# x's first 512 rows loaded as row pairs and transposed as even and odd tiles, with one filler slot fewer, in a dense GELU forward and backward kernel

## The chip, the cores and the metric

The kernel runs on one core of one Trainium2 chip. The metric is the device time of one execution in microseconds (us); a time of a kernel is the median of several runs. A profiled execution also gives a span, from the first to the last instruction of the program.

## The reference

A dense layer with tanh-GELU, its output, and the gradients of all five inputs for a given `grad_out`:

```python
def _fwd_reference(x, w1, b1, w2, b2):
    h = jnp.einsum("bsd,df->bsf", x, w1) + b1
    h = jax.nn.gelu(h, approximate=True)
    return jnp.einsum("bsf,fd->bsd", h, w2) + b2
# B, S, D, F = 1, 2048, 448, 1792, all bf16
# outputs: out, and the vjp at grad_out: dx, dw1, db1, dw2, db2
```

## The kernel before

The 2048 rows of x are worked in 4 blocks of 512 rows, the 1792 hidden columns in 14 tiles of 128, two of which form a pair; so there are 28 pairs (block, two hidden tiles). For each pair TensorE (PE) computes u = (x w1) transposed, VectorE (DVE) and ScalarE (ACT) add the bias and make GELU and its derivative, PE computes q = (grad_out w2^T) transposed, DVE multiplies the two. PE also makes the rows of the output (`o`) and of dx (`x`) from earlier pairs. When all pairs are done, PE computes dw1 (line 843) and dw2 (line 897) with full-height matmuls; everything before runs as two half-height matmuls of 64 rows side by side, a slot (line 246).

The order on every engine is written out by hand, in the strings `PE_ORDER`, `ACT_ORDER`, `DVE_ORDER` and `SP_ORDER`. A planner (`Plan`) walks these five lists and emits an instruction when all that it needs has been emitted; the waits themselves are put in afterwards by the framework, from the memory that each instruction reads and writes, in the order of emission.

The first 512 rows of x need to stand transposed in `xT[0]`, 64 columns of edge and then one column for each row of x. For the other blocks a transposing DMA does that. For the first block the rows are loaded plainly (`LXN`, tokens `xr..`, into the tile `TR2`), PE transposes them by a matmul with an identity (`XT`, tokens `X0` to `X3`, four slots each, into the PSUM banks 0 to 3), and DVE and ACT copy the results out of PSUM into `xT[0]` (`XC`, line 637). A token `X2.1` in `DVE_ORDER` or `ACT_ORDER` is the copy of tile 2, half 1; a half is 64 of the tile's 128 rows. Tiles 0 and 2 use banks 0 and 1, tiles 1 and 3 use banks 2 and 3, so X2 can't be transposed before the copies of X0 are done.

PE's program begins

```python
W6 X0 X1 F6 X2 X3 S0 B T1 u1.1 h1.2 u1.2 u2.1 ...
```

- `W6`: six matmuls of 512 columns on a constant (line 393), which need no data.
- `X0 X1`: transposes of tiles 0 and 1.
- `F6`: six slots of 128 columns on a constant (`fill`), which write PSUM banks that nobody reads.
- `X2 X3`: transposes of tiles 2 and 3.
- `S0`: pair 0's u for columns 0 to 255 of the block, 14 matmuls of 256 columns in 7 slots. It reads the columns of xT that tiles 0 and 1 fill, and the first part of w1.
- `B`: a small matmul that turns b1 (line 711). DVE copies its result (token `b1T`, line 736), and all bias additions need it.
- `T1`: pair 0's u for columns 256 to 511, first half of its sum, in two pieces of 128 columns. It reads what tiles 2 and 3 fill.

The loads are issued at the very start: tile 0 on SP's queue (`xr01`), tile 1 on ACT's (`xr12`), tiles 2 and 3 together on SP's (`xr24`), then parts of w1 on both.

Where ACT and DVE share the copies: DVE has X0.0, X1.0, X2.1, X3.1, ACT has X0.1, X1.1, X2.0, X3.0.

Of the kernel before, what the change touches and what calls it, by code (L numbers as in the profile page):

```python
# [88 lines left out]


PE_ORDER = """
W6 X0 X1 F6 X2 X3 S0 B T1 u1.1 h1.2 u1.2 u2.1 u3.1 u2.2 u3.2 p0.0 p0.1 p0.2 p0.3 p1.0 p1.1 p1.2 u4.1 u5.1 u4.2
u5.2 p1.3 p2.0 p2.1 p2.2 p2.3 u6.1 p3.0 u6.2 p3.1 p3.2 p3.3 p4.0 p4.1 u7.1 p4.2 u7.2 p4.3 p5.0 p5.1 p5.2 p5.3 u8.1
p6.0 u8.2 q0.1 p6.1 q0.2 u9.1 p6.2 u9.2 q1.1 p6.3 q1.2 u10.1 o1.0.0.6.1 u10.2 q2.1 o1.1.0.6.1 u11.1 q2.2 u11.2
o1.0.0.6.2 o1.1.0.6.2 q3.1 u12.1 q3.2 u12.2 o1.0.6.10.1 q4.1 o1.1.6.10.1 u13.1 q4.2 u13.2 o1.0.6.10.2 q5.1 o1.1.6.10.2
# [43 lines left out]
@with_exitstack  # L139
def kernel(  # L140
    ctx: ExitStack,
    tc: tile.TileContext,
    x: bass.AP,
    w1: bass.AP,
    b1: bass.AP,
    w2: bass.AP,
    b2: bass.AP,
    grad_out: bass.AP,
    out_0: bass.AP,
    out_1: bass.AP,  # L150
    out_2: bass.AP,
    out_3: bass.AP,
    out_4: bass.AP,
    out_5: bass.AP,
):
    pl = make_plan(tc, ctx, x, w1, b1, w2, b2, grad_out, out_0, out_1, out_2, out_3, out_4, out_5)
    with tc.manual_schedule():
        pl.emit()


def make_plan(tc, ctx, x, w1, b1, w2, b2, grad_out, out_0, out_1, out_2, out_3, out_4, out_5):
    nc = tc.nc
    P = 128
    _, S, D = x.shape
# [5 lines left out]
    EDGE = 64  # L170
    sc = math.sqrt(GELU_C * GELU_A)

    x2 = x.rearrange("b s d -> (b s) d")
# [19 lines left out]
    xT = [sb.tile([P, 4, EDGE + SB], BF16, name=f"xT{i}") for i in range(2)]  # L193
# [9 lines left out]
    NUB, NUX, NTR = 3, 14, 3  # L203
    ub_t = [sb.tile([P, 2, SB], BF16, name=f"ub{i}") for i in range(NUB)]
    ub_x = [gh_nat[:, NB - 1 - i // NPB, 2 * (i % NPB):2 * (i % NPB) + 2, :, :].rearrange("p f s c -> p f (s c)") for i in range(NUX)]
    TR = [sb.tile([P, 2, 2, SB], BF16, name=f"TR{i}") for i in range(NTR)]
# [10 lines left out]
    def bk_(i):  # L217
        return BK[i][:, :] if i < 6 else qb[:, i - 6, :]
# [8 lines left out]
    def bk16(i):  # L227
        return bk_(i)[:, 0:D].bitcast(BF16)
# [186 lines left out]
    def val(v, place):  # L415
        if v not in pl.place:
            pl.put(v, place)
        return v
# [135 lines left out]
    def dq(eng):  # L554
        return {"SP": nc.sync, "ACT": nc.scalar, "POOL": nc.gpsimd}[eng]
# [4 lines left out]
    def dma(eng, name, out, in_, reads, writes, nbytes):  # L560
        def fn():
            d = loads[name] = dq(eng).dma_start(out=out, in_=in_)
            if name in HOLD:
                tc.add_manual_dep(d.ins, loads[HOLD[name]].ins.name, DEP, reason="behind the identity")
        pl.op(eng, name, fn, list(reads) + (["ident"] if name in HOLD else []), writes, ("dma", nbytes, "plain"))
# [27 lines left out]
        pl.op("DVE", f"edge{tag}", lambda: nc.vector.tensor_copy(out=dst[64:128, 3, EDGE - 1:EDGE], in_=dst[0:64, 0, EDGE:EDGE + 1]),  # L593
              [(tag, 0, 0)], [v], ("tiny", 1))

    x_rows = TR[NTR - 1][:, :, :, :].rearrange("p a h s -> p (a h) s")
    ident = stage[0][:, 0, 0:P]
    nums, turned, nums128 = stage[1][:, 0, 0:16], stage[1][:, 0, 32:64], stage[1][:, 0, 128:256]
    row, block = [stage[1][:, 1, 2 * i:2 * i + 2].bitcast(F32) for i in (0, 1)]

    def LXN(t0, t1, eng="SP"):

        src = x2[t0 * P:t1 * P, :].rearrange("(t p) d -> p t d", p=P)
        dma(eng, f"xrows{t0}", x_rows[:, t0:t1, 0:D], src, [], [("xrows", t) for t in range(t0, t1)], (t1 - t0) * 114688)

    def identity():

# [24 lines left out]
        pe(f"xt{t}", fn, [("xrows", t), "ident"], [bank(("xt", t, i), bks[i]) for i in (0, 1)], ("s64", 4), (bks, 0))  # L632

    def XC(t, i, eng):
        out = xT[0][:, :, EDGE + t * P + 64 * i:EDGE + t * P + 64 * i + 64]
        src = bk16(X_BANKS[t][i])[:, 0:256].rearrange("p (k s) -> p k s", k=4)
        fn = (lambda: nc.scalar.copy(out=out, in_=src)) if eng == "ACT" else (lambda: nc.vector.tensor_copy(out=out, in_=src))
        pl.op(eng, f"xc{t}.{i}", fn, [("xt", t, i)], [val(("xT", 0, t // 2), ("xT", 0, t // 2))], ("copy", 256))
# [56 lines left out]
    def num(t):  # L695
        return [int(i) for i in t.split(".")]

    for t in PE_ORDER.split():
        k, a = t[0], t[1:]
# [15 lines left out]
        elif k == "h":  # L715
            hf, d = num(a)
# [7 lines left out]
        else:  # L724
            b, half, f0, f1, d = num(a)
# [13 lines left out]
    for eng, order in (("ACT", ACT_ORDER), ("DVE", DVE_ORDER)):  # L739
        for t in order.split():  # L740
            k, a = t[0], t[1:]
            if k == "k":
                CS(0, "AB".index(a[-1]))
            elif k == "c":
                hf = None if a[-1] in "AB" else int(a[-1])
                a = a if hf is None else a[:-1]
                C(int(a[:-1]), "AB".index(a[-1]), eng, hf)
            elif k == "v":
                EV(a[0], *num(a[1:]), eng)
            elif k == "L":  # L750
                LW1(int(a), eng)
            elif k == "Z":
                LW1Z(int(a), eng)
            elif t[:2] == "xr":
                LXN(int(t[2]), int(t[3]), eng)
            elif t == "ident":
                pl.op(eng, "ident", identity, ["identz"], ["ident"], ("tiny", 1))
            elif k == "X":
                XC(*num(a), eng)
            elif k == "D":  # L760
                LED({"x": "xT", "g": "gT"}[a[0]])
            elif k == "K":
                LW2(int(a), eng)
            elif t in ("b1", "b2"):
                (LB1 if t == "b1" else LB2)(eng)
            elif t == "b1T":
                pl.op(eng, "b1T", b1_turn, [("b1u",)], ["b1T"], ("tiny", 4))
            elif t == "table":
                pl.op(eng, "table", lambda: nc.scalar.activation(out=tiny[:], in_=one[:, 0:1], func=ACT.Gelu_apprx_tanh), [], ["tiny"], ("table", 1))
            else:  # L770
                step[k](int(a))
# [7 lines left out]
    for t in SP_ORDER.split():  # L779
        k, a = t[0], t[1:]  # L780
        if t[:2] == "xr":
            LXN(int(t[2]), int(t[3]), "SP")
        elif k in "XY":
            b, *hs = num(a)
            LX(*((x2, xT, "xT") if k == "X" else (g2, gT, "gT")), b, hs or [0, 1])
        elif k in "RF":
            (LW1R if k == "R" else LW1F)()
        elif t in ("b1", "b2"):
            (LB1 if t == "b1" else LB2)("SP")
        elif t in ("L1a", "L1b"):  # L790
            LW1(1, "SP", *((0, 2) if a[-1] == "a" else (2, 3)))
        elif k in "LZKJI":
            {"L": LW1, "Z": LW1Z, "K": LW2, "J": LW2T, "I": LW1T}[k](int(a))
        elif k == "E":
            LE("SP")
        elif k in "HT":
            {"H": HS, "T": GHT}[k](int(a))
        elif k == "S":
            ST(a[0], *num(a[1:]))
        elif t == "Nx":  # L800
            rows_nat("xn", x_nat, x2, [("w1", i) for i in range(len(W1_COLS))] + ["w1r", "w1f"])
        elif t == "Ng":
            rows_nat("gn", g_nat, g2, [("w2T", i) for i in range(4)])
# [34 lines left out]
    for ft in range(NF):  # L838
# [7 lines left out]
        eng = "ACT"  # L846
        dst, src = w_stage[ft % (4 * NTR)][:, 0:D], bk_(bk)[:, 0:D]
# [4 lines left out]
        c = ft // 4  # L852
# [37 lines left out]
    for ft in range(NF):  # L890
        halves = [(0, D)] if ft < NF - 1 else [(0, D - P), (D - P, D)]
        for (d0, d1) in halves:
# [7 lines left out]
            dst, src = gw2_sb[:, ft, d0:d1], bk_(bk)[:, 0:d1 - d0]  # L900
            eng = "DVE" if (ft % 2 == 1 and ft < NF - 1) else "ACT"
# [39 lines left out]
```

## Time and profile before

| | us |
|---|---|
| median of 3 runs | 263.89 |
| lowest, highest run | 263.8, 264.7 |
| the profiled execution, its own time | 264.0 |
| its span | 262.2 |
| PE busy in the span | 258.8 |
| DVE busy | 199.0 |
| ACT busy | 127.7 |

The two timestamps that matter are inside the first 7 us: the transposes of x begin at 3.41 us of the span, and the first real matmuls of u at 4.89 us. From there to the end PE always has an instruction in work. Ends of matmuls in the profile are modelled, and one matmul's end lies beyond the start of the next, so the pace of PE is read from starts.

### The profile page before, as it was taken

Reading aid. Unit: us, or ns where it says so; the run is one execution under the profiler, and the core shown is the slowest. Engines: PE = TensorE matmul, PEld = TensorE weight load, DVE = VectorE, ACT = ScalarE, POOL = GpSimd, SP = SyncE. Lnnn points to the kernel's source line nnn. Section 1 sums busy time; section 2 is a strip of 40 time slices with the busy share of each in tenths; the row PEclk is TensorE's granted clock in tenths of the full one; section 3 lists DMA queues with packets and bytes.
Section 4 is the critical chain, followed back from the end, with each engine's and each line's share of the span. In section 5 each row is a group of like instructions: output and inputs, shape, how many; then the busy total and the mean of one; then the engine's idle time right before and its main releaser. Section 6 shows DMA issues by size and latency. Waiting matters only on the chain.

```text
span 262.2 us, 5414 instructions
## 1 busy us (share of the span) xinstructions
PE 258.8 (99%) x2217; PEld 148.2 (57%) x2217; DVE 199.0 (76%) x287; ACT 127.7 (49%) x166; POOL 14.2 (5%) x11
## 2 busy tenths in 40 slices
PE   8999999999999999999999999999999999999995
PEld 5544455555555666666666676765555555555554
DVE  4998398999989989999997995249999999310000
ACT  4899569936898956875896310011121111000001
POOL 1000000000000000000000000000000392400000
DMA  7999989999999982972488725875899799974221
GB/s 211 287 262 161 196 130 198 249 338 223 254 180 232 254 179 43 193 206 43 109 201 258 214 42 63 249 221 116 176 212 174 157 231 153 232 158 128 72 70 35
DMA packets 120617, 46.61 MB, mean 178 GB/s; under 512 B 96670, under 2 KB 120463, under 8 KB 120592
## 3 DMA queue, kind: packets, MB, share of 16 engines
q1 hardware_dynamic: 119904, 45.82, 77.3%
q10 hardware_dynamic: 688, 0.44, 0.5%
q8 instruction: 17, 0.28, 0.4%
q14 instruction: 8, 0.07, 0.1%
HBM read 8.20 MB, written 14.28 MB: 86 GB/s over the span
## 4 chain that ended last, share of the span: by engine, by line
PE 99%; ACT 0%; issue 0%
PE bank L246 48%; PE qb L246 18%; PE bank L843 16%; PE bank L897 16%; PE qb L393 1%; ACT w_sb L902 0%; PE bank L711 0%
## 5 line engine op out<-in xcount | busy, mean ns | idle before, releaser
L246 PEld LDWEIGHTS <-HG 64*128 64x128 bf16 x896 | 54.7, 94 | 33.1 <-POOLq L239 2.1
L246 PE MATMUL qb<-gT,w2Tf 64*128 64x512 bf16 x392 | 52.8, 376 | 0.0
L246 PE MATMUL bank<-w_sb,HG 64*128 64x448 bf16 x448 | 48.3, 349 | 0.0
L246 PE MATMUL bank<-xT,w1f 64*128 64x512 bf16 (+2 forms) x361 | 47.2, 367 | 0.0
L246 PE MATMUL bank<-w1T_sb,HG 64*128 64x448 bf16 x448 | 47.2, 349 | 0.0
L519 DVE SCALAR_TENSOR_TENSOR HG<-TR,qb 128x1024 bf16<-128x1024 bf16 x28 | 34.1, 1216 | 12.6 <-PE qb L246 12.6
L897 PE MATMUL bank<-w2Tf,HG 128*128 128x448 bf16 (+2 forms) x240 | 42.6, 340 | 0.0
L843 PE MATMUL bank<-w1f,gh_nat 128*128 128x448 bf16 x224 | 42.5, 352 | 0.0
L897 PEld LDWEIGHTS <-HG 128*128 128x128 bf16 x240 | 22.9, 98 | 19.8
L843 PEld LDWEIGHTS <-gh_nat 128*128 128x128 bf16 x224 | 21.8, 98 | 20.6 <-issue 0.4
L246 PEld LDWEIGHTS <-w2Tf 64*128 64x128 bf16 x392 | 23.6, 94 | 17.1 <-POOLq L239 0.3
L504 ACT ACTIVATE TR<-TR 128x1024 bf16<-128x1024 bf16 x28 | 29.2, 1052 | 6.6 <-DVE TR L494 6.6
L246 PEld LDWEIGHTS <-w1f 64*128 64x128 bf16 x388 | 22.1, 95 | 16.9 <-POOLq L239 0.7
L866 DVE TENSOR_TENSOR w1T_sb<-w1T_sb,gh_nat 128x1792 f32<-128x1792 f32 x14 | 28.4, 2026 | 0.5
L848 ACT ACTIVATE TR<-bank 128x448 bf16<-128x448 f32 x14 | 7.6, 544 | 34.9 <-PE bank L843 34.9
L903 DVE CAST w_sb<-bank 128x448 bf16<-128x448 f32 x6 | 3.7, 624 | 25.9 <-PE bank L897 25.9
L902 ACT CAST w_sb<-bank 128x448 bf16<-128x448 f32 (+2 forms) x9 | 4.4, 491 | 37.7 <-PE bank L897 37.7
L872 POOL PARTITION_ALL_REDUCE w1T_sb<-w1T_sb x1 | 10.6, 10568 | 205.9 <-DVE w1T_sb L870 205.9
L479 ACT ACTIVATE TR<-gh_nat 128x1024 bf16<-128x1024 bf16 x15 | 15.7, 1052 | 11.5 <-DVE TR L514 11.5
L509 DVE TENSOR_SCALAR TR<-TR 128x2048 bf16<-128x2048 bf16 x28 | 19.1, 687 | 1.9 <-ACT TR L504 1.9
L499 DVE TENSOR_TENSOR TR<-TR,HG 128x1024 bf16<-128x1024 bf16 x28 | 19.1, 682 | 0.0
L514 DVE TENSOR_TENSOR TR<-TR 128x1024 bf16<-128x1024 bf16 x28 | 19.0, 684 | 0.1
(54 smaller groups left out, 190.4 us busy)
## 6 DMA issues: line engine op xcount, KB each, us to landing
hT_dram<-HG SPq DMA_DIRECT2D x28, 256.0 KB, 3.1
out_dram<-st SPq DMA_DIRECT2D x16, 224.0 KB, 3.1
w1f<-in_x_dram SPq DMA_DIRECT2D x2, 896.0 KB, 5.8
w2Tf<-in_grad_out_dram SPq DMA_DIRECT2D x1, 1792.0 KB
out_dram<-w_sb SPq DMA_DIRECT2D x2, 448.0 KB, 3.0
out_dram<-xT SPq DMA_DIRECT2D x2, 384.0 KB, 3.8
w_sb<-in_w_dram SPq DMA_DIRECT2D x1, 672.0 KB
w1f<-in_w_dram SPq DMA_DIRECT2D x3, 192.0 KB, 3.6
```

What stands on the lines that cost most here:

```text
L246: m = nc.tensor.matmul(out, lhsT=l, rhs=r, start=st, stop=sp, skip_group_check=True, is_transpose=turn or None)
L479: pl.op("ACT", f"s{p}", lambda: nc.scalar.activation(out=TR[p % NTR][:, 1], in_=ubuf(p), func=ACT.Square, scale=sc), [("ub", p)], [v], ("a ...
L499: pl.op("DVE", f"R{p}", lambda: nc.vector.tensor_tensor(out=t[:, 1], in0=t[:, 1], in1=hblk(p), op=ALU.mult), [("r", p), ("h", p)], [val((" ...
L504: pl.op("ACT", f"t{p}", lambda: nc.scalar.activation(out=t[:, 0], in_=t[:, 0], func=ACT.Tanh), [("y", p)], [val(("t", p), ("TR0", p % NTR) ...
L509: pl.op("DVE", f"m{p}", lambda: nc.vector.tensor_scalar(out=t[:], in0=t[:], scalar1=1.0, scalar2=None, op0=ALU.subtract), [("t", p), ("r2" ...
L514: pl.op("DVE", f"n{p}", lambda: nc.vector.tensor_tensor(out=t[:, 0], in0=t[:, 0], in1=t[:, 1], op=ALU.mult), [("m0", p), ("m1", p)], [val( ...
L519: pl.op("DVE", f"G{p}", lambda: nc.vector.scalar_tensor_tensor(out=ghblk(p), in0=t[:, 0], scalar=2.0, in1=qb[:, :, :], op0=ALU.subtract, o ...
L843: nc.tensor.matmul(bk_(bk)[:, 0:D], lhsT=gh_nat[:, st // 4, ft, st % 4, :], rhs=x_nat[:, st, :], start=(st == 0), stop=(st == NS - 1))
L848: fn = (lambda dst=dst, src=src: nc.scalar.mul(out=dst, in_=src, mul=-0.5)) if eng == "ACT" else \
L866: nc.vector.tensor_tensor(out=hs3, in0=a, in1=gh_nat[:, st // 4, :, st % 4, :], op=ALU.add)
L872: pl.op("POOL", "gb1", lambda: nc.gpsimd.partition_all_reduce(gb1_w, hsum, channels=P, reduce_op=bass_isa.ReduceOp.add), ["hsc"], ["gb1"], ...
L897: nc.tensor.matmul(bk_(bk)[:, 0:d1 - d0], lhsT=h_nat[ft][:, st, :], rhs=g_nat[:, st, d0:d1], start=(st == 0), stop=(st == NS - 1))
```

## The change

The loads of x's first 512 rows take two neighbouring rows of x to one partition: 896 elements that lie side by side in DRAM, in one piece. The first load now fills partitions 0 to 63 with rows 0 to 127 of x, the second partitions 64 to 127 with rows 128 to 255, the third all 128 partitions with rows 256 to 511. Tile 0 is thereby the even rows of x's rows 0 to 255 and tile 1 the odd ones; tiles 2 and 3 are the even and the odd rows of 256 to 511. A transposed tile is copied to every second column of `xT[0]`: 64 columns, two elements apart. The half i of a tile now holds the rows of the i-th 128 of its 256. And `F6` becomes `F5`.

```diff
-W6 X0 X1 F6 X2 X3 S0 B T1 u1.1 h1.2 u1.2 ...
+W6 X0 X1 F5 X2 X3 S0 B T1 u1.1 h1.2 u1.2 ...
...
-    x_rows = TR[NTR - 1][:, :, :, :].rearrange("p a h s -> p (a h) s")
+    x_rows = TR[NTR - 1][:, :, :, :].rearrange("p a h s -> p (a h s)")[:, 0:4 * D].rearrange("p (t d) -> p t d", t=4)
...
     def LXN(t0, t1, eng="SP"):

-        src = x2[t0 * P:t1 * P, :].rearrange("(t p) d -> p t d", p=P)
-        dma(eng, f"xrows{t0}", x_rows[:, t0:t1, 0:D], src, [], [("xrows", t) for t in range(t0, t1)], (t1 - t0) * 114688)
+        h, ps = (1, slice(0, P)) if t0 == 2 else (0, slice(64 * t0, 64 * t1))
+        src = x2[2 * P * h:2 * P * (h + 1), :].rearrange("(p t) d -> p t d", t=2)
+        dma(eng, f"xrows{t0}", x_rows[ps, 2 * h:2 * h + 2, :], src[ps], [], [("xrows", 2 * h), ("xrows", 2 * h + 1)], (t1 - t0) * 114688)
...
     def XC(t, i, eng):
-        out = xT[0][:, :, EDGE + t * P + 64 * i:EDGE + t * P + 64 * i + 64]
+        c = EDGE + 2 * P * (t // 2) + P * i + t % 2
+        out = xT[0][:, :, c:c + P - 1:2]
```

On PE, between the transposes of tiles 1 and 2, the end of the fill (`const` is the constant, `TR` the loaded rows of x, `st` the identity):

```order
 L246 LDWEIGHTS const-bfloat16-1.0
 L246 MATMUL qb<-const-bfloat16-1.0 128x128
-L246 LDWEIGHTS const-bfloat16-1.0
-L246 MATMUL qb<-const-bfloat16-1.0 128x128
-L246 LDWEIGHTS const-bfloat16-1.0
-L246 MATMUL qb<-const-bfloat16-1.0 128x128
 L246 LDWEIGHTS TR_80
 L246 MATMUL bank_89<-st_81,TR_80 128x64
```

One slot, two matmuls of 128 columns with their weight loads, is gone; nothing else on PE changes its place.

On DVE, the four copies out of PSUM, X0.0, X1.0, X2.1 and X3.1, and b1's copy behind them, with the engines that each waits for (bank 89 is bank 0, 90 is 1, 91 is 2, 92 is 3). Before:

```order
L637 COPY xT_68<-bank_89 128x4x64 [waits PE_49]
L637 COPY xT_68<-bank_91 128x4x64 [waits PE_49]
L637 COPY xT_68<-bank_90 128x4x64 [waits PE_49,Activation_49]
L637 COPY xT_68<-bank_92 128x4x64 [waits PE_49,Activation_49]
L736 COPY b1T<-bank_94 128x16 [waits PE_49]
```

With the change:

```order
L639 COPY xT_68<-bank_89 128x4x64 [waits PE_49]
L639 COPY xT_68<-bank_91 128x4x64 [waits PE_49]
L639 COPY xT_68<-bank_90 128x4x64 [waits PE_49,Activation_49]
L639 COPY xT_68<-bank_92 128x4x64 [waits Activation_49]
L738 COPY b1T<-bank_94 128x16 [waits PE_49]
```

The places are the same, but the copy of X3.1 no longer waits for PE by itself: the wait of the copy ahead of it already covers it. In the built program the copy of X2.1 waited for the count of PE's semaphore that the last transpose of X2 brings; now it waits for the count that the last matmul of `S0` brings, which stands behind both X2 and X3.

On ACT, the copies X0.1, X1.1, X2.0, X3.0 and the first bias addition. Before:

```order
L637 COPY xT_68<-bank_90 128x4x64 [waits PE_49]
L637 COPY xT_68<-bank_92 128x4x64 [waits PE_49]
L637 COPY xT_68<-bank_89 128x4x64 [waits DVE_49,PE_49]
L637 COPY xT_68<-bank_91 128x4x64 [waits DVE_49,PE_49]
L459 ACTIVATE HG<-qb,b1T 128x256 [waits DVE_49]
```

With the change:

```order
L639 COPY xT_68<-bank_90 128x4x64 [waits PE_49]
L639 COPY xT_68<-bank_92 128x4x64 [waits PE_49]
L639 COPY xT_68<-bank_89 128x4x64 [waits DVE_49,PE_49]
L639 COPY xT_68<-bank_91 128x4x64 [waits DVE_49]
L459 ACTIVATE HG<-qb,b1T 128x256 [waits DVE_49]
```

The same has moved here: the copy of X2.0 waits for the count that the last matmul of `S0` brings, and the copy of X3.0 for nothing further of PE. Two more waits differ on PE: X0 waits for both the first and the second load (before, X0 for the first and X1 for the second), and the first matmul of `T1` waits for ACT's copy X3.0 (before, for X2.0).

More of the change, by code (lines that the diff above doesn't have):

```diff
@@ L91 @@
 PE_ORDER = """
-W6 X0 X1 F6 X2 X3 S0 B T1 u1.1 h1.2 u1.2 u2.1 u3.1 u2.2 u3.2 p0.0 p0.1 p0.2 p0.3 p1.0 p1.1 p1.2 u4.1 u5.1 u4.2
+W6 X0 X1 F5 X2 X3 S0 B T1 u1.1 h1.2 u1.2 u2.1 u3.1 u2.2 u3.2 p0.0 p0.1 p0.2 p0.3 p1.0 p1.1 p1.2 u4.1 u5.1 u4.2
 u5.2 p1.3 p2.0 p2.1 p2.2 p2.3 u6.1 p3.0 u6.2 p3.1 p3.2 p3.3 p4.0 p4.1 u7.1 p4.2 u7.2 p4.3 p5.0 p5.1 p5.2 p5.3 u8.1
```

## Prediction

> **What bounds the kernel now.** I read the page first, then the waits of PE, then the timeline of the first 7 us, engine by engine. From the page and the waits of PE (engine, line, what it waited for: us in total, times, longest):
>
> ```profile
> span 262.2 us, 5414 instructions
> ...
> PE 99%; ACT 0%; issue 0%
> ...
> PE qb L393 <- PEq L925: 0.8, 1, 0.8
> ```
>
> The chain that ended last is PE in 99%, and PE's only idle stretch is the 0.8 us before its first instruction. So there is no later stall in which a delay of the first microseconds could disappear: a microsecond that PE loses at the start is lost at the end, and one that it gains is gained. The timeline of PE over the change's place (start us, us, engine, line, operation, count):
>
> ```profile
> 0.76 2.72 PE L393 MATMUL qb<-const-bfloat16-1.0 128*128 128x512 bf16 x6 [0.76 <-PEq L925]
> 3.41 0.61 PE L246 MATMUL bank<-st,TR 64*128 64x64 bf16 x16
> 3.83 0.83 PE L246 MATMUL qb<-const-bfloat16-1.0 64*128 64x128 bf16 x12
> 4.45 0.64 PE L246 MATMUL bank<-st,TR 64*128 64x64 bf16 x16
> 4.89 0.51 PE L246 MATMUL qb<-xT,w1f 64*128 64x256 bf16 x4
> 5.24 0.49 PE L246 MATMUL bank<-xT,w1f 64*128 64x256 bf16 x6
> 5.56 0.27 PE L246 MATMUL bank<-xT,gh_nat 64*128 64x256 bf16 x2
> 5.67 0.27 PE L246 MATMUL qb<-xT,w1f 64*128 64x256 bf16 x1
> 5.68 0.27 PE L246 MATMUL qb<-xT,gh_nat 64*128 64x256 bf16 x1
> 5.78 0.17 PE L711 MATMUL bank<-st,b1n 64*128 64x16 bf16 x1
> 5.79 0.35 PE L246 MATMUL bank<-xT,w1f 64*128 64x128 bf16 x6
> ```
>
> Row by row these are W6, X0 and X1, F6, X2 and X3, S0 (4.89 to 5.68, 14 matmuls in 7 slots), B, and the start of T1 at 5.79. Starts give the pace. F6's six slots of 128 columns take 4.45 - 3.83 = 0.62 us, 0.103 each. S0's two first slots of 256 columns take 5.24 - 4.89 = 0.35, 0.175 each, its next three 5.56 - 5.24 = 0.32, 0.107 each. PE's pace doubles inside S0, at about 5.1 us. The column of the granted clock doesn't show this; it stands at 1.00 where the pace is the slow one (window, its length, busy us and count of PE, PEld, DVE, ACT, POOL, granted clock, DMA share, GB/s):
>
> ```profile
> 3.40:4.90 1.50, 1.50 (x47) 1.50 (x47) 0.50 (x2) 0.94 (x4) 0.00 (x0) 1.00 1.07 326
> ```
>
> **The slot.** F5 for F6 takes one slot of 0.103 us out of the slow stretch. X2 would start at 4.45 - 0.10 = 4.35, S0 at 4.79. If the pace still doubles at 5.1 whatever PE does, S0 does 0.31 us of its work before that at 0.206 a slot (twice the 0.103), that is 1.5 slots, and the other 5.5 at 0.107: its last slot is issued out at 5.69 instead of 5.78, and about half to all of the slot is gained: I take **-0.09 us at the end of S0**. Nothing but the slot stood in the way only if the copies of X0 and X1 and the third load are ready 0.1 us sooner; both come next.
>
> [...] The trace agrees with a fixed moment no better than with one that moves with the work; one profile can't show it.
>
> **The loads.** Issues and landings (the three loads of TR; KB each, us from issue to landing; then the issues):
>
> ```profile
> TR<-in_x_dram SPq DMA_DIRECT2D x1, 224.0 KB, 3.2
> TR<-in_x_dram ACTq DMA_DIRECT2D x1, 112.0 KB, 2.7
> TR<-in_x_dram SPq DMA_DIRECT2D x1, 112.0 KB, 2.5
> ...
> 0.72 0.40 ACTq L562 DMA_DIRECT2D TR<-in_x_dram  x1
> ...
> 1.17 0.42 SPq L562 DMA_DIRECT2D TR<-in_x_dram  x1
> ...
> 2.84 0.63 PE L393 MATMUL qb<-const-bfloat16-1.0 128*128 128x512 bf16 x1
> ```
>
> ACT's load lands at 0.72 + 2.7 = 3.4, SP's first at 3.2, the third at 1.17 + 3.2 = 4.4. X0 started at 3.41; from now on it needs ACT's load too, which lands at just that time. Half as many pieces, twice as long, the same bytes: I expect landings as before. Sooner, X0 can't start before W6's last matmul is issued out, 2.84 + (2.84 - 0.76)/5 = 3.26, so 0.15 us is the most that is gained. Later: loads of 64 partitions stand elsewhere in the trace,
>
> ```profile
> w1f<-in_w_dram SPq DMA_DIRECT2D x2, 224.0 KB, 3.7
> ```
>
> 3.7 us for 224 KB, where the third load of TR took 3.2 for as much over 128 partitions. Half of that difference for half of the bytes is 0.25 us. I take 0, with -0.15 and +0.25 as ends, and the third load the same: at 4.4 it is as late as X2's new start, 4.35, so 0.05 us of the slot may remain a wait.
>
> [...]
>
> **The copies.** Copies out of PSUM by ACT and DVE, and what stands behind them:
>
> ```profile
> 3.87 0.65 ACT L637 COPY xT<-bank 128x256 bf16<-128x256 bf16 x2 [0.16 <-PE bank L246]
> 4.90 0.65 ACT L637 COPY xT<-bank 128x256 bf16<-128x256 bf16 x2 [0.39 <-PE bank L246]
> ...
> 3.83 0.50 DVE L637 COPY xT<-bank 128x256 bf16<-128x256 bf16 x2 [0.95 <-PE bank L246]
> 5.00 0.50 DVE L637 COPY xT<-bank 128x256 bf16<-128x256 bf16 x2 [0.67 <-PE bank L246]
> 6.00 0.17 DVE L736 COPY b1T<-bank 128x16 f32<-128x16 f32 x1 [0.49 <-PE bank L711]
> ...
> 6.21 0.84 ACT L459 ACTIVATE HG<-qb,b1T 128x256 f32<-128x256 f32 x2 [0.66 <-DVE b1T L736]
> ...
> L246 PE MATMUL bank<-st,TR x32: 230/238/258, 3.4 to 4.8; 64*128 64x64 bf16 x32
> ```
>
> No row shows a write to every second column. The number of elements is the same, 256 to a partition, so I take the same 0.65 for ACT's two and 0.50 for DVE's two. The lower end is no change; the upper is ACT's pair of as many elements with twice the bytes on both sides (L459), 0.84, +0.19 us for the two.
>
> **The new wait is the large term.** X2's four slots take 0.055 us each ((4.89 - 4.45)/8), so the last starts at 4.62 and, at 0.24 a matmul, ends at 4.86. ACT's copy X2.0 starts at 4.90, 0.04 later, DVE's X2.1 at 5.00, 0.14 later: both run while PE does S0. In the changed program both wait for S0's last matmul. That one started at 5.68 and lasted 0.27, end 5.95; with the slot gone, 5.86. So ACT starts at 5.90 and ends its second copy at 5.90 + 0.65 = 6.55; DVE starts at 6.00 and ends at 6.50. T1's first matmul waits for ACT's second copy, and with the 0.04 of a signal starts at about 6.59. It started at 5.79. Between S0 and T1 PE has only B, which needs 0.1 us; it stands still from about 5.7 to 6.6, and nothing in PE's order can go past T1. The shift is **6.59 - 5.79 = +0.80 us**, with the slot's gain already in it.
>
> Queued behind the held copies are b1T on DVE and the bias additions on ACT. ACT is free at 6.55, b1T starts at about 6.45 rather than 6.00, and L459 at about 6.65 rather than 6.21: 0.45 us late, while PE is 0.80 late. So these engines gain distance on PE and don't add a second wait.
>
> **Sum.** The profiled execution took 264.0, 0.1 above the median of 263.89. 264.0 + 0.80 = 264.8; from the median 264.7, which I forecast. Ends: loads -0.15 to +0.25, copies 0 to +0.19, the doubling of the pace another 0.05 either way.
>
> **Rivals.**
>
> - *The load takes the lead.* The two loads of 64 partitions land 0.25 us late and X0 with them; everything above shifts by up to that: 264.95. For it: X0 now needs both. Against it: the bytes and the queues are the same. 12 in 100.
> - *The wait isn't one (not slower).* The copies go on as before because the count they wait for is reached already by X3's transposes; then T1 starts 0.09 earlier than before, and the time is 263.8. It decides at 5.0: a first copy on ACT that starts before 5.0 is through (0.65) before S0 and B are issued out at about 5.7, and PE isn't held. For it: the order shows engines waited for and the same rows as before in all but two. Against it: two copies have lost a wait of their own for X3's end, which only a later wait ahead of them can replace. 8 in 100.
> - *The pause delays the double pace.* PE ran 5.1 - 0.76 = 4.3 us before its pace doubled. In the profiled execution that is before the new pause of 0.9 us, but in a run in which it comes after 5.7 the pause lies ahead of it. If PE then had to work 4.3 us anew from 6.6, the pace would double at 10.9, and half of 6.6 to 10.9 would be lost: +2.15, 266.9. The spread of the runs before, 263.8 to 264.7, would fit a doubling that comes up to 2 x 0.9 = 1.8 us later in some runs. 10 in 100 for the median.
>
> [...]
>
> **How the numbers follow.** The forecast has 68 in 100, the rivals 12, 8 and 10; the last 2 are for a time more than 0.5% lower, for which I have no mechanism. Forecast and late loads, with their ends, cover 264.1 to 265.4: 8 in 10. A measurement of this kernel can tell about 0.5%, 1.3 us, from no change: slower than 265.2 are the delayed doubling and 4 in 100 of the upper ends, together 0.14; faster 0.02; the rest, 0.84, within.
>
> **What would show it.** In the profile of the changed kernel: the second pair of copies on ACT and DVE starts behind S0's last matmul, near 5.9 and 6.0 instead of 4.9 and 5.0; PE gets a new idle entry of about 0.9 us before T1 on L246, put down to ACT; T1 starts near 6.6; F5 to X2 is 0.1 us shorter; the pairs of copies still take 0.65 and 0.50. It is wrong if T1 starts before 6.2 (the wait isn't there), if X0 starts after 3.6 (the loads), or if the slots of 512 columns after T1 still run at 0.4 us (the pace).

## The result, and the profile after

The changed kernel takes 268.55 us (median of 6 runs, 265.98 to 268.9), the kernel before beside it 264.1 (6 runs, 263.8 to 264.7). The ratio is 1.0151 (95% interval 1.0111 to 1.019): slower, and past the upper end of the forecast range. Five of the six runs lie at 268.34 to 268.9, one at 265.98. The profiled execution took 268.52, against the 264.0 of before: 4.52 us to be found.

The page of the changed kernel, and the waits of PE (engine, line, what it waited for: us in total, times, longest):

```profile
span 266.7 us, 5407 instructions
...
PE 97%; DMA 2%; ACT 0%; SPq 0%; issue 0%
...
PE bank L246 <- DMA TR<-in_x_dram: 1.0, 2, 0.8
PE bank L246 <- ACT xT L639: 0.8, 1, 0.8
PE qb L393 <- PEq L927: 0.8, 1, 0.8
```

PE is still the chain that ended last, but where it had waited once, it now waits four times: twice for the loads of x and once for ACT's copies besides the start. These three come to 1.8 us, not half of the loss. The rest has to be in PE's own pace, and that is read from starts. The timeline of PE (start us, us, engine, line, operation, count, idle before it by modelled ends and what ended it):

```profile
0.76 2.72 PE L393 MATMUL qb<-const-bfloat16-1.0 128*128 128x512 bf16 x6 [0.76 <-PEq L927]
3.75 0.61 PE L246 MATMUL bank<-st,TR 64*128 64x64 bf16 x16 [0.27 <-DMA TR<-in_x_dram]
4.17 0.72 PE L246 MATMUL qb<-const-bfloat16-1.0 64*128 64x128 bf16 x10
5.64 0.61 PE L246 MATMUL bank<-st,TR 64*128 64x64 bf16 x16 [0.75 <-DMA TR<-in_x_dram]
6.06 0.61 PE L246 MATMUL qb<-xT,w1f 64*128 64x256 bf16 x4
...
7.54 0.22 PE L713 MATMUL bank<-st,b1n 64*128 64x16 bf16 x1
8.59 0.50 PE L246 MATMUL bank<-xT,w1f 64*128 64x128 bf16 x6 [0.83 <-ACT xT L639]
...
9.39 1.51 PE L246 MATMUL bank<-xT,w1f 64*128 64x512 bf16 x6
10.67 0.66 PE L246 MATMUL bank<-xT,gh_nat 64*128 64x512 bf16 x2
...
11.74 1.02 PE L246 MATMUL bank<-xT,w1f 64*128 64x512 bf16 x5
...
12.60 0.82 PE L246 MATMUL qb<-xT,w1f 64*128 64x512 bf16 x6
13.25 0.39 PE L246 MATMUL qb<-xT,gh_nat 64*128 64x512 bf16 x2
```

Down the rows: W6, X0 with X1, F5, X2 with X3, S0, B, T1. X0 starts at 3.75 (3.41 before). F5's five slots of 0.103 us are issued out at 4.68, and X2 comes at 5.64: 0.96 us of pause, where before there was none. B is issued at 7.54 and T1 starts at 8.59, 1.04 later. And the pace: the three slots of 512 columns from 9.39 to 10.67 take 0.427 each, those from 12.60 to 13.25 take 0.217. Between 11.74 and 12.60 lie one slow and two fast ones (0.427 + 2 x 0.217 = 0.86), so the pace doubled at about 12.17 us. Before, it doubled at 5.17.

The copies out of PSUM on ACT as timeline rows, and those on DVE and ACT in the view by source line (count, ns of the shortest, the median and the longest copy, first and last start). The two rows of L637 are those of before:

```profile
4.21 0.75 ACT L639 COPY xT<-bank 128x256 bf16<-128x256 bf16 x2 [0.22 <-PE bank L246]
7.79 0.75 ACT L639 COPY xT<-bank 128x256 bf16<-128x256 bf16 x2 [2.83 <-PE bank L713]
...
L639 DVE COPY xT<-bank x4: 431/438/442, 4.2 to 8.2; 128x256 bf16<-128x256 bf16 x4
L639 ACT COPY xT<-bank x4: 442/442/443, 4.2 to 8.1; 128x256 bf16<-128x256 bf16 x4
...
L637 DVE COPY xT<-bank x4: 290/292/292, 3.8 to 5.2; 128x256 bf16<-128x256 bf16 x4
L637 ACT COPY xT<-bank x4: 372/374/378, 3.9 to 5.2; 128x256 bf16<-128x256 bf16 x4
```

The second pair starts at 7.79, behind S0's and B's matmuls, as the order of the built program had said; before, it started at 4.90, 0.04 us behind X2. ACT needs 0.75 for two instead of 0.65, DVE 0.78 instead of 0.50.

The loads of x's first rows (KB, us from issue to landing) and their issues on SP:

```profile
TR<-in_x_dram SPq DMA_DIRECT2D x1, 224.0 KB, 4.2
TR<-in_x_dram SPq DMA_DIRECT2D x1, 112.0 KB, 3.0
TR<-in_x_dram ACTq DMA_DIRECT2D x1, 112.0 KB, 2.5
...
1.38 0.80 SPq L562 DMA_DIRECT2D TR<-in_x_dram  x1
```

The load of 224 KB, which spans all 128 partitions as before, is issued 0.2 us later, its issue takes 0.80 instead of 0.42, and it takes 4.2 to land instead of 3.2: it is there at 5.6 us, not at 4.4. X2 waits for it.

### The profile page after: what moved, and what is told of

Same layout as the page of the kernel before. It is cut to its first block, busy times and chain, and to the rows that moved or that the text cites. A ratio compares the mean times of both kernels' runs of the same rounds, so it can differ in the third digit from the quotient of the medians.

```text
span 266.7 us, 5407 instructions
## 1 busy us (share of the span) xinstructions
PE 261.4 (98%) x2215; PEld 156.8 (59%) x2215; DVE 199.5 (75%) x287; ACT 127.9 (48%) x166; POOL 14.2 (5%) x11
## 4 chain that ended last, share of the span: by engine, by line
PE 97%; DMA 2%; ACT 0%; SPq 0%; issue 0%
PE bank L246 47%; PE qb L246 17%; PE bank L845 16%; PE bank L899 16%; DMA TR<-in_x_dram 2%; ACT xT L639 0%; SPq L562 0%; ACT w_sb L904 0%; PE bank L713 0%
## 5 line engine op out<-in xcount | busy, mean ns | idle before, releaser
L246 PEld LDWEIGHTS <-HG 64*128 64x128 bf16 x896 | 58.7, 94 | 29.1 <-POOLq L239 2.0
L246 PE MATMUL bank<-xT,w1f 64*128 64x512 bf16 (+2 forms) x361 | 49.5, 380 | 0.8 <-ACT xT L639 0.8
L246 PEld LDWEIGHTS <-w1f 64*128 64x128 bf16 x388 | 24.6, 99 | 17.5 <-issue 1.0
L246 PEld LDWEIGHTS <-w2Tf 64*128 64x128 bf16 x392 | 25.5, 94 | 15.2 <-POOLq L239 0.3
```

Source lines behind the costliest of these rows:

```text
L246: m = nc.tensor.matmul(out, lhsT=l, rhs=r, start=st, stop=sp, skip_group_check=True, is_transpose=turn or None)
```

## The experiments

The theory after these rows: two late loads (0.34 us ahead of X0, 0.96 ahead of X2) and the hold ahead of T1 (1.04) are the visible half, and the pauses together keep the double pace away until 12.2 us, which is the other half. The rival: the pace changes by chance of the execution, and the pauses alone are the effect. Each kernel is compared with runs of before on the same chip; their medians were 264.09 to 264.45. Three points in a listing stand for lines that aren't shown.

**The slot alone** (kernel before with F5):

```diff
-W6 X0 X1 F6 X2 X3 S0 B T1 ...
+W6 X0 X1 F5 X2 X3 S0 B T1 ...
```

> The kernel before with F5 in place of F6, nothing else. Theory (the slot is worth what the prediction gave it, at most 0.1 us): 264.0 against 264.1, no difference that can be told; X2 starts at 4.35 to 4.45 of the span, the pace doubles near 5.1 as before. [...]

264.34 us (10 runs), ratio 1.0007 (0.9997 to 1.0018). One filler slot fewer is worth nothing that shows.

**The loads alone** (kernel before with the change's three loads and the plain copies):

```diff
...
-        src = x2[t0 * P:t1 * P, :].rearrange("(t p) d -> p t d", p=P)
-        dma(eng, f"xrows{t0}", x_rows[:, t0:t1, 0:D], src, ...)
+        h, ps = (1, slice(0, P)) if t0 == 2 else (0, slice(64 * t0, 64 * t1))
+        src = x2[2 * P * h:2 * P * (h + 1), :].rearrange("(p t) d -> p t d", t=2)
+        dma(eng, f"xrows{t0}", x_rows[ps, 2 * h:2 * h + 2, :], src[ps], ...)
```

> The kernel before (F6, copies to neighbouring columns, no hold) with the new loads alone. Since the copies are not spread, block 0's columns stand in another order and its rows come out permuted. Theory (pauses ahead of the doubling make it late): the loads land as in the changed kernel, near 3.7 and 5.6, X0 starts near 3.75, X2 near 5.64, T1 1.2 us late, and the pace doubles near 8.6 or later instead of 5.1; 1.2 us of pauses and at least 1.2 of slow pace: 266.5 or more. Rival 1 (the doubling does not care for pauses): only the pauses, 265.2. Rival 2 (the late landing was chance of one execution): landings 3.2 to 3.4 and 4.3, time 264.1.

265.73 us (10 runs), ratio 1.0054 (1.0027 to 1.0081), and the runs form two groups: five at 264.54 to 265.03, five at 266.43 to 267.01. The profile, of a run in the upper group: waits of PE, loads, and PE's timeline where the pace changes:

```profile
PE bank L246 <- DMA TR<-in_x_dram: 0.9, 2, 0.5
...
TR<-in_x_dram SPq DMA_DIRECT2D x1, 224.0 KB, 4.2
...
8.42 1.06 PE L246 MATMUL bank<-xT,w1f 64*128 64x512 bf16 x6
9.31 0.39 PE L246 MATMUL bank<-xT,gh_nat 64*128 64x512 bf16 x2
```

The lateness is the loads' own, with no hold and no spread copies in the program. Three slots of 512 take 0.89 here, one slow and two fast: the pace doubles at 8.84, not at 5.17. The two groups lie some 2 us apart with the same instructions in both; the 266.5 or more that was expected is the upper group, the median is below it.

**The copies alone** (kernel before, F6, with the spread copies; they bring the hold along):

```diff
-        out = xT[0][:, :, EDGE + t * P + 64 * i:EDGE + t * P + 64 * i + 64]
+        c = EDGE + 2 * P * (t // 2) + P * i + t % 2
+        out = xT[0][:, :, c:c + P - 1:2]
```

> The kernel before (old loads, F6) with the spread copies alone, which brings the hold of the copies of X2 and X3 until S0's end. Block 0's rows come out permuted. Theory: S0 ends at 5.95, the copies take 0.44 each, T1 starts near 6.8 instead of 5.8; the pause lies behind the doubling at 5.1 and does not move it: 264.1 + 1.0 = 265.1. Rival (the hold is what costs the double pace): a doubling near 10 or later, 267 or more.

265.36 us (6 runs, 264.77 to 265.59), ratio 1.0044 (1.0031 to 1.0057). PE's timeline at T1:

```profile
6.21 0.17 PE L712 MATMUL bank<-st,b1n 64*128 64x16 bf16 x1
7.22 0.34 PE L246 MATMUL bank<-xT,w1f 64*128 64x128 bf16 x6 [0.83 <-ACT xT L638]
```

The hold stands here without the new loads, 1.0 us from B to T1. The data don't ask for it: S0 reads columns 0 to 255, and the held copies fill columns 256 to 511. The spread target alone brings it, since nothing else was changed; why the framework then puts the wait in is not shown. The pace had already doubled, at 6.05, and the runs form one group. Of the 1.44 us that this execution takes more than before, 1.00 are the pause, its own length and no more; the rest is a doubling at 6.05 instead of 5.17, which lies ahead of the pause and so can't come from it.

**The hold without the spread copies** (kernel before; the copies of X2 made to wait for S0's last matmul by hand, and those of X3 stand behind them on their engines):

```diff
...
+            c = nc.scalar.copy(out=out, in_=src) if eng == "ACT" else nc.vector.tensor_copy(out=out, in_=src)
+            if t == 2:
+                tc.add_manual_dep(c.ins, loads["S0"].ins.name, DEP, reason="held")
```

> The kernel before with the hold alone: the copies of X2 wait for S0's last matmul by a wait put in by hand; loads, copies and slot as before. Theory (hold and longer copies are two terms of the 1.3 us of the spread copies): S0 ends at 5.95, ACT's two copies take 0.65, T1 starts near 6.6, +0.8, 264.9. Rival (the hold is all of it, the copies' length is hidden): 265.4, as with the spread copies.

264.99 us (10 runs), ratio 1.0017 (1.0005 to 1.0029). PE's timeline at T1:

```profile
5.54 0.17 PE L717 MATMUL bank<-st,b1n 64*128 64x16 bf16 x1
6.17 0.34 PE L246 MATMUL bank<-xT,w1f 64*128 64x128 bf16 x6 [0.46 <-ACT xT L641]
```

The pause is 0.62 us. With plain copies T1's first piece of 128 columns is tile 2 alone and needs only the first of ACT's two copies; the expectation counted both. With the spread copies the same columns are filled from tiles 2 and 3, so T1 needs both of ACT's copies, each slower. That is what makes the hold 1.0 in the change.

**A pause ahead of everything** (kernel before with three waking matmuls fewer):

```diff
-W6 X0 X1 F6 X2 X3 S0 B T1 ...
+W3 X0 X1 F6 X2 X3 S0 B T1 ...
```

> The kernel before with W3 in place of W6: PE stands still from about 2.0 to 3.4, its work begins at the same 3.4, and less is asked of it. [...]

265.15 us (10 runs, 264.47 to 266.01, evenly spread and not in two groups), ratio 1.0028 (1.0012 to 1.0043). PE's timeline, X0 and the place where the pace doubles:

```profile
3.25 0.61 PE L246 MATMUL bank<-st,TR 64*128 64x64 bf16 x16 [1.05 <-DMA TR<-in_x_dram]
...
7.07 0.94 PE L246 MATMUL bank<-xT,w1f 64*128 64x512 bf16 x6
7.83 0.39 PE L246 MATMUL bank<-xT,gh_nat 64*128 64x512 bf16 x2
```

X0 starts 0.16 us earlier than before and nothing behind it waits, yet the kernel is slower: the pace doubles at 7.31. Less work and an earlier start, but a pause ahead, and a later doubling. This is the pace by itself.

**Half the partitions without the longer pieces** (kernel before; the first two loads over 64 partitions each, in pieces of 896 bytes, one row):

```diff
...
+        h, ps = (1, slice(0, P)) if t0 == 2 else (0, slice(64 * t0, 64 * t1))
+        src = x2[2 * P * h:2 * P * (h + 1), :].rearrange("(t p) d -> p t d", t=2)
+        dma(eng, f"xrows{t0}", x_rows[ps, 2 * h:2 * h + 2, :], src[ps], ...)
```

> The kernel before with loads of 64, 64 and 128 partitions as in the changed kernel, but a partition's two rows lie 128 rows apart in x, so each piece is 896 bytes as before. Block 0's rows come out permuted; copies and F6 as before. Theory (the length of the pieces makes the loads late): landings as before, 3.2 to 3.5 and 4.3, 264.1 to 264.4. Rival (64 partitions make them late): landings near 3.7 and 5.5, 265.7 as with the new loads.

Other than the expectation says, the rows keep their natural order in this kernel, and nothing of the computation is changed. 266.25 us (6 runs: three at 265.31 to 265.52, three at 266.97 to 267.14), ratio 1.0071 (1.0042 to 1.0101). Its loads, the third load's issue, and the waits of PE:

```profile
TR<-in_x_dram SPq DMA_DIRECT2D x1, 224.0 KB, 4.7
...
1.55 0.80 SPq L562 DMA_DIRECT2D TR<-in_x_dram  x1
...
PE bank L246 <- DMA TR<-in_x_dram: 1.6, 2, 0.9
```

The third load is here the very load of before, 128 partitions in pieces of one row. Its issue takes 0.80 instead of 0.42 and its landing 4.7 instead of 3.2. What differs is that two loads ahead of it went to 64 partitions each; its rows also lie closer together in the tile, as they do in the next kernel. The narrowed loads' own issues take longer too: 0.77 us on SP and 0.73 on ACT, where before they took 0.39 and 0.40 (in the change 0.60 and 0.56). And their data come late: in slices of 0.225 us, the first bytes of any queue move in the slice from 1.58 us before, and in the one from 2.03 here, in the change and with the loads alone. Up to 2.4 us, SP's queue had moved 84 packets before and none in the change. So the first load's delay is there before its data move.

**The longer pieces without half the partitions** (kernel before; row pairs, 1792 bytes, in two loads of 128 partitions, one on each queue):

```diff
...
+        if t0 == 2:
+            return
+        h = t0
+        src = x2[2 * P * h:2 * P * (h + 1), :].rearrange("(p t) d -> p t d", t=2)
+        dma(eng, f"xrows{t0}", x_rows[:, 2 * h:2 * h + 2, :], src, ...)
```

> The kernel before with row pairs in pieces of 1792 bytes, but in two loads of 128 partitions: rows 0 to 255 on SP's queue, rows 256 to 511 on ACT's. Block 0's rows come out permuted; copies and F6 as before. Theory (the length of the pieces makes the loads late): both loads are issued in 0.8 instead of 0.4 and land near 4 or later; X0 starts at 4 or later; 265 or more. Rival (64 partitions make them late): issue 0.4, X0 near 3.5, 264.1.

264.49 us (10 runs), ratio 1.0003 (0.9992 to 1.0015). Its loads, and a wait of PE that no other kernel here has:

```profile
TR<-in_x_dram SPq DMA_DIRECT2D x1, 224.0 KB, 2.9
TR<-in_x_dram ACTq DMA_DIRECT2D x1, 224.0 KB, 3.1
...
PE qb L246 <- DMA w1f<-in_w_dram: 0.6, 1, 0.6
```

Row pairs cost nothing that shows in the time. The loads are issued in 0.39 and 0.41 us, and the first bytes move in the slice from 1.58 us, as before. (The profiled execution, at 264.8, isn't without losses: X0 starts 0.27 late, and PE stands 0.8 for a part of w1 behind the doubling, which came early, at 4.46.) The theory that the longer piece makes the loads late has fallen; the 64 partitions do it.

**Nine filler slots more, ahead of X2** (the changed kernel with F14), and **a seventh waking matmul and eight slots more** (the changed kernel with W7 and F13):

```diff
-W6 X0 X1 F5 X2 X3 S0 B T1 ...
+W6 X0 X1 F14 X2 X3 S0 B T1 ...
...
+W7 X0 X1 F13 X2 X3 S0 B T1 ...
```

> The changed kernel with F14 in place of F5: nine more filler slots of 0.107, which fill the pause ahead of X2 and delay nothing if X2's load lands at 5.6. Theory (PE's pause makes the doubling late): more work on PE and less time; the pace doubles near 5.3 or 8.6 instead of 12.2, T1 stays near 8.3, 268.55 less at least 1.7: 266.8 or lower. Rival (the doubling does not depend on the pause, or the hold's pause alone decides it): 268.5, the same.

> The changed kernel with W7 for W6 and F13 for F5: the pauses ahead of X0 and ahead of X2 are both filled, the hold stays. Theory (pauses ahead of the doubling make it late): as with F14 alone or a little below, 265.5 to 266.0, all runs in one group; the doubling before 7. Rival (the gain of F14 was the one slot's place, or chance): 268.5.

265.8 us (4 runs, 265.73 to 266.02), ratio 1.0066 (1.0051 to 1.0081), and 265.93 us (4 runs, 265.7 to 266.15), ratio 1.0067 (1.0052 to 1.0082). With more work in PE's program they are 2.75 and 2.6 us faster than the change. All eight runs lie at 265.7 to 266.15, where one of the change's six does: were the pace a matter of chance alone, as the rival has it, eight of eight would be unlikely beside one of six. Chance has a part in it, as the single runs that fall out of their groups show, but the pauses set the odds. PE's timeline of the second, its fill and T1:

```profile
4.35 1.14 PE L246 MATMUL qb<-const-bfloat16-1.0 64*128 64x128 bf16 x26
5.49 0.41 PE L246 MATMUL bank<-st,TR 64*128 64x64 bf16 x16
...
7.51 0.34 PE L246 MATMUL bank<-xT,w1f 64*128 64x128 bf16 x6 [0.84 <-ACT xT L639]
```

The thirteen slots start 0.10 us apart up to 4.86 and 0.06 from there: the pace doubles at 4.85, and X2's matmuls are fast (0.41 for the row instead of 0.61). The hold ahead of T1 is as long as ever, 1.0. In the profile of F14 the pace had doubled before X0, ahead of the added slots, so that one profile says nothing for the fill; the eight runs do.

**Nine filler slots in the hold** (the changed kernel with nine slots of 128 columns between B and T1):

```diff
-W6 X0 X1 F5 X2 X3 S0 B T1 ...
+W6 X0 X1 F5 X2 X3 S0 B V9 T1 ...
...
+        elif k == "V":
...
```

> The changed kernel with nine more filler slots behind B, ahead of T1, which fill the hold's pause; F5 and the pause ahead of X2 stay. Theory (the hold's pause is what spoils the second chance): the doubling comes near 8.8 at the latest instead of 12.2, and the time falls to two groups, near 266 and near 267.5. Rival (only the pause ahead of X2 decides): 268.5, the same.

267.44 us (4 runs: three at 267.44 to 267.57, one at 265.82), ratio 1.0106 (1.0069 to 1.0142): 1.1 us faster than the change. The two intervals overlap, but three of the four runs lie 0.77 us and more below the lower end of the change's group of five. T1 starts when it can, at 8.36, so the slots cost hardly a wait; the pace doubles at 10.19 instead of 12.17, later than the 8.8 that was expected:

```profile
9.17 1.32 PE L246 MATMUL bank<-xT,w1f 64*128 64x512 bf16 x6
10.32 0.39 PE L246 MATMUL bank<-xT,gh_nat 64*128 64x512 bf16 x2
```

**The loads and the hold without the spread copies** (the second and the fourth edit together, F6):

> The kernel before with the new loads and with the hold put in by hand; plain copies to neighbouring columns, F6. Block 0's rows come out permuted. Theory (the pause of the loads spoils the doubling, the pause of the hold spoils the next chance too): most runs near 268.3 as in the changed kernel, the doubling after 11. Rival (the pauses add up without that): the loads' 265.7 and the hold's 0.6, 266.3, in two groups near 265.4 and 267.3.

267.12 us (4 runs: three at 267.06 to 267.23, one at 265.6), ratio 1.0099 (1.0069 to 1.0129). The median falls between the two expectations, but the two groups, and a doubling at 9.62 rather than after 11, are what the rival said: the pauses add up. Its pauses are 0.65 ahead of X0 (0.13 of it stood there before), 0.65 ahead of X2 and 0.66 ahead of T1. Loads alone gave 1.0054 and this hold alone 1.0017; the interval doesn't exclude their sum. So no run shows that this shorter hold delays the doubling further; three of four runs in the upper group instead of five of ten are too few to tell. PE's timeline where the pace doubles:

```profile
9.02 1.11 PE L246 MATMUL bank<-xT,w1f 64*128 64x512 bf16 x6
9.96 0.38 PE L246 MATMUL bank<-xT,gh_nat 64*128 64x512 bf16 x2
```

**The change with its loads mended** (the changed kernel with the row pairs loaded over 128 partitions, in two loads; nothing is left out):

```diff
-        h, ps = (1, slice(0, P)) if t0 == 2 else (0, slice(64 * t0, 64 * t1))
+        if t0 == 2:
+            return
+        h = t0
...
-        dma(eng, f"xrows{t0}", x_rows[ps, 2 * h:2 * h + 2, :], src[ps], ...)
+        dma(eng, f"xrows{t0}", x_rows[:, 2 * h:2 * h + 2, :], src, ...)
```

> The changed kernel (F5, spread and held copies) with its row pairs loaded over 128 partitions in two loads, rows 0 to 255 on SP's queue and 256 to 511 on ACT's; nothing is left out. Theory (the loads of 64 partitions make the pauses that cost the double pace; hold and spread copies cost 1.3 by themselves): X0 near 3.7, X2 without a wait for its load, the doubling before 7 in all runs, 265.4 to 265.9. Rival (the spread copies with the slot gone cost the double pace as well): 267 or more.

265.39 us (6 runs, 265.26 to 265.82), ratio 1.0041 (1.0028 to 1.0055). The waits of PE:

```profile
PE bank L246 <- ACT xT L641: 0.8, 1, 0.8
...
PE bank L246 <- DMA TR<-in_x_dram: 0.4, 1, 0.4
```

The wait ahead of X2 is gone, the hold stands, and the pace doubles at 6.21. X0 starts at 3.87, later than the 3.7 that was expected. This is the best form of the change that was run, 3.2 us faster than the change and about what the copies alone cost; it doesn't beat the kernel before, and no kernel here does.

## Why the prediction was wrong

All of these kernels differ in the first 13 us only, so a profiled execution can be added up. PE loses the time that it stands idle, and half of the time that it works at the slow pace, since that work would take half as long at the other (0.217 us a slot of 512 columns instead of 0.427). Idle time and slow work (from 0.76 us to the doubling, less the idle time in it) are read from starts; before they are 0.13 and 4.28 us. Slots added or left out count at the double pace.

| kernel | pace doubles at | idle, added | half of the slow work added | slots | sum | its own time less 264.0 |
|---|---|---|---|---|---|---|
| the change | 12.17 | 2.34 | 2.33 | -0.05 | 4.62 | 4.52 |
| loads alone | 8.84 | 1.21 | 1.23 | 0 | 2.44 | 2.43 |
| copies alone | 6.05 | 1.00 | 0.44 | 0 | 1.44 | 1.44 |
| hold alone | 4.6 | 0.62 | -0.27 | 0 | 0.35 | 0.43 |
| W3 | 7.31 | 1.12 | 0.51 | -0.64 | 0.99 | 0.95 |
| loads and hold | 9.62 | 1.83 | 1.31 | 0 | 3.14 | 3.06 |
| nine slots in the hold | 10.19 | 1.14 | 1.94 | 0.43 | 3.51 | 3.44 |
| W7 and F13 | 4.85 | 1.27 | -0.21 | 0.58 | 1.64 | 1.70 |
| mended loads | 6.21 | 1.55 | 0.24 | -0.05 | 1.74 | 1.82 |

In no row is more than 0.1 us left unexplained. (Not in the table: the slot alone, -0.05 by this sum and as measured; the longer pieces, 0.7 against 0.8; and F14 and the half partitions, whose pace doubled somewhere inside a pause, ahead of X0 and ahead of X2.) By the prediction's own steps:

- **What bounds the kernel** held: PE, and every microsecond lost at the start is lost at the end.
- **The slot**, -0.09: nothing that can be measured, 1.0007. The 0.05 either way that the sum has for the doubling is shown by no run; the profiles show it at 5.17 us before and at 12.17 in the change.
- **The loads are the step that failed.** "Half as many pieces, twice as long, the same bytes: I expect landings as before", ends -0.15 and +0.25, "and the third load the same". X0 came 0.34 late, a little past the upper end, because SP's narrowed load took 3.0 us to land instead of 2.5 (ACT's took 2.5 instead of 2.7). The larger miss is the third load, which the change hardly touches: it came 1.2 late, and X2 waited 0.96 for it. What was missed is that the narrowed loads delay the load behind them, and the runs on half the partitions and on the longer pieces show that the 64 partitions cause it and the piece's length doesn't. The prediction took its price from landings alone; the two loads of 64 partitions that it looked at took 0.6 us each to issue, and the loads of TR about 0.4. Inside the queue the mechanism stays open: the runs show that the issues take longer (in the change 0.60 and 0.56 us instead of 0.39 and 0.40), that the first data come late (from 2.04 instead of 1.68) and that the next load lands later (5.6 instead of 4.4), not why.
- **The copies**, 0 with +0.19 at most: +0.10 for ACT's pair, inside the bounds. (DVE's pair took 0.28 more, but T1's start waited for ACT's.)
- **The hold** was right in kind: the copies start behind S0's last matmul, and PE stands still before T1, put down to ACT. Forecast was a pause of 0.9 us; it is 1.0 where it stands alone, the 0.1 being the slower copies, and 1.04 in the change.
- **The pause that delays the double pace** was a rival with 10 in 100, and it is half of the loss: 2.33 of 4.62. But the trigger was mis-stated. The prediction tied it to the hold alone and reckoned 266.9. The hold alone doesn't do it (one group of runs each, 1.0044 and 1.0017); the loads alone do it in half of the runs; the whole change does it in five of six, and to 12.17 instead of 8.84. So the rival should have had all the pauses ahead of the doubling in it, the loads' first, and its chance hung on the load term that had been set at nothing. That the narrowed loads decide it is shown: with the loads mended the doubling comes at 6.21 and the time falls to 265.39. That the hold then adds a further delay of the doubling rests on the run with nine slots in it alone, and the run with the loads and a shorter hold doesn't bear it out.
- **The wait isn't one**, 8 in 100: it is.

How a pause of 1 us can delay the doubling by 3 to 7 is shown only in part. With the same instructions, runs of the loads alone, of the half-partition loads and of the loads with the hold lie in two groups 1.5 to 2 us apart. By the loss of half of the slow time, that is a doubling 3 to 4 us earlier or later, an estimate from these times. The profiles have shifts of that size: from 5.17 before to 8.84 with the loads alone, 3.67, and from there to 12.17 in the change, 3.33. They have other moments too (7.31, 9.62, 10.19), and the ten runs of W3 are spread evenly, so a step of one size is not shown. Nor did any run measure how much idle time ahead puts the doubling off, or why it does. That the loads' pauses delay the doubling (8.84 instead of 5.17), and that filler work in them brings it back (4.85 with W7 and F13, and eight runs at 265.7 to 266.15), is shown.

## What to carry to other kernels

Where PE is the bound, don't cost a new pause ahead of the pace's doubling at its own length: read from starts where the pace doubles, and look at all the pauses ahead of that together, since in these runs they decided whether half of another few microseconds went too (2.33 us in the change). A late load in the first microseconds can then be worth covering with useless matmuls: here nine slots won 2.75 us back. And when a load is narrowed to part of the partitions, look at the load queued behind it, not only at the narrowed one (here it landed at 5.6 us instead of 4.4); and when a copy's target becomes a spread one, look at who counts as a reader of it (here it brought a pause of 1.0 us).

## What the runs showed of the hardware

- Two loads over 64 partitions each, issued ahead, lengthened the issue of an unchanged load of 224 KB from 0.42 to 0.80 us and its landing from 3.2 to 4.7; their own issues took 0.77 and 0.73 instead of 0.39 and 0.40. Two loads of 224 KB over 128 partitions, in pieces twice as long, were issued in 0.39 and 0.41 and landed after 2.9 and 3.1.
- A copy of 256 elements out of PSUM to every second column takes DVE 0.44 us instead of 0.29, ACT 0.44 instead of 0.37, for the same elements and bytes.
- The granted clock is 1.00 in every profiled execution here, at the slow pace of 0.427 us a slot of 512 columns as at 0.217.
- Fewer waking matmuls made X0 start earlier (3.25 against 3.41); the 1.05 us of idle time ahead of it are put down to its load. In the kernel before, W6 is issued out at about 3.27, and some 0.13 us lie between the last full-height matmul and the first half-height one. So X0 very likely didn't wait for its load there; one profile of W3 shows it, and what the 0.13 us are is not shown.
